# Sparse attention feeding a Sinkhorn-gated mixture of experts: the first batch's rounds with a step's values beside its transposes, eight rounds in place of nine, and half of the first weight pieces split inside the expert's first slots

## The chip, the cores and the metric

The kernel runs on one core of a Trainium2 chip. The metric is the device time of one execution in microseconds (us). Engines are named as in the profile: PE is TensorE (PEld its weight loads), DVE is VectorE, ACT is ScalarE, POOL is GpSimd, SP is the engine whose queue issues the DMAs.

## The reference, cut to what matters

```python
# attention: 4 batches, 8 heads, 576 positions, head_dim 64
scores = scale * q @ k.T
# heads 0..3: rel = i - j in 0..31;  heads 4..7: rel >= 0 and i % 32 == j % 32
attn = softmax(where(mask, scores, -1e9))        # rows divided by (sum + 1e-9)
x = (attn @ v) as [2304, 512]
# mixture of experts, E = 8, F = 1024
P = exp(x @ w_gate - max); 8 times: rows to 1, columns to 1, times N / E
out = sum over e of P[:, e:e+1] * (relu(x @ w1[e]) @ w2[e])
```

## The kernel before

**Attention in steps.** A batch of attention is eight steps: a pair of heads and a part of the positions. `STEPS` gives the order. Steps 0 to 3 of a batch are strided heads (in turn 4 and 6 blocks of scores, in two PSUM tiles, one for each head of the pair), steps 4 and 5 are local heads with four windows (positions 0 to 255), steps 6 and 7 local heads with five windows (positions 256 to 575). There are 32 steps. `at_k` counts rounds. A step k passes through four stages, each in another round:

- `at_scores` (line 195): score matmuls on PE, mask, scale and row minimum on DVE (L237), exponentials with row sums on ACT (L243).
- `at_normalize` (line 249): two short DVE instructions on the sums (L252, L253), then the multiplication on POOL (L255).
- `at_transpose` (line 259): transposes on PE (L267) into PSUM tiles of tag "t", then a DVE copy to `pt` (L268).
- `at_values` (line 271): values matmuls on PE (L280, L294), then for each piece the upper half of the result by ACT (L313) and the lower half by DVE (L314) into `reg`, the input x of the expert layers in two parts.

**Order.** The schedule is manual: each engine runs its instructions in the order in which the program emits them. Before the expert starts, nine rounds run for the first batch (lines 727 to 732). Round k emits scores of step k, values of step k - 3 (`LAG`), transposes of step k - 2, normalizing of step k - 1; the values round also issues the loads of step k + 2 on SP's queue. Rounds 1 to 8 each end with `split_w` of one weight piece: an ACT copy (L165), a POOL subtraction (L166), and the load of the next piece on SP's queue (four `raw` buffers). Four pieces are loaded ahead of the rounds.

**Slots.** Then the expert runs in slots (line 775): `layer1` of 256 tokens for a quarter of an expert's half (twelve PE matmuls, L389; relu on ACT and DVE, L395, L396) and `layer2` of the slot before (L413). As long as attention steps are left, a slot also holds one attention round, with the values in a PSUM tile of tag "t". `layer1` of slots 0 to 3 reads positions 0 to 255, so steps 0 to 5 of the first batch; slot 4 is the first that reads positions beyond them (steps 6 and 7). After the attention come gating, the second half of expert 0 and seven further experts (from about 250 us to the end).

```python
for k in range(2 * NP - 2 + LAG):
    attention_scores()
    attention_values("l1")
    attention_rest()            # transposes of at_k - 2, normalizing of at_k - 1
    if 1 <= k <= 2 * FH:
        split_w(*plain[k - 1])
```

Of the kernel before, what the change touches and what calls it, by code (L numbers as in the profile page):

```python
# [55 lines left out]
def kernel(  # L56
# [9 lines left out]
    nc = tc.nc  # L66
    P = 128
    NT, D = out.shape
    E, _, F = w1.shape
    NDT = D // P  # L70
    NP = NDT
    NTT = NT // P
    FH = 4
# [28 lines left out]
    cst = const.tile([P, 4, P], F32, name="cst")  # L102
# [45 lines left out]
    def load_w():  # L148
        nonlocal n_loaded
        if n_loaded == len(plain):  # L150
            return
        u, ft, which = plain[n_loaded]
        n_loaded += 1
        e, fh = divmod(u, UPE)
        f0 = (fh * FH + ft) * P
        t = raw_p.tile([P, D], F32, tag="raw", name=f"raw{which}_{u}_{ft}")
        if which == 0:
            t = t.rearrange("p (k f) -> p k f", f=P)
            nc.sync.dma_start(t, w1[e, :, f0 : f0 + P].rearrange("(k p) f -> p k f", p=P))
        else:  # L160
            load_w2(t, e, f0)
        raw[u, ft, which] = t
# [5 lines left out]
    def split_w(u, ft, which):  # L168
        src = raw.pop((u, ft, which))
        if which == 0:  # L170
            t = pools["w1"].tile([P, 2, NDT, P], F32R, tag="w1", name=f"w1_{u}_{ft}")
        else:
            t = w2_p.tile([P, 2, D], F32R, tag="w2", name=f"w2_{u}_{ft}")
        split(t[:, 0], t[:, 1], src)
        wt[u, ft, which] = t
        load_w()
# [5 lines left out]
    NS = len(steps)  # L182
    QK = -(-max(sum(_columns(*x)[:2]) for x in STEPS) // P) * P
    qkv_t, sms, sums_t, pts = {}, {}, {}, {}

    def load_qkv(k):
        if k < NS:
            nq, nk, nv = _columns(*steps[k][1:])
            t = pools["qkv"].tile([P, QK], F32, tag="qk", name=f"qk_{k}", bufs=3)
            nc.sync.dma_start(t[:, : nq + nk], qkv[k, :, : nq + nk])  # L190
            tv = pools["qkv"].tile([P, 5 * 2 * DH], F32, tag="v", name=f"v_{k}", bufs=5)
            nc.sync.dma_start(tv[:, :nv], qkv[k, :, nq + nk : nq + nk + nv])
            qkv_t[k] = t, tv[:, :nv].rearrange("p (w j d) -> p w j d", j=2, d=DH)
# [65 lines left out]
    def at_transpose(k):  # L259
        pts[k] = []  # L260
        for j, (sm, _, n, rows, nk) in enumerate(sms.pop(k)):
            pt = pools["qkv"].tile([P, 5, P], F32, tag="pt", name=f"pt_{k}_{j}", bufs=4)
            for i0 in range(0, n, 4):
                m = min(4, n - i0)
                tp = ps.tile([P, 4, P], F32, tag="t", name=f"tp_{k}_{j}_{i0}")
                for i in range(m):
                    nc.tensor.transpose(tp[:nk, i, :rows], sm[:, i0 + i, :], ident[:rows, :rows])  # L267
                nc.vector.tensor_copy(pt[:nk, i0 : i0 + m, :rows], tp[:nk, :m, :rows])  # L268
            pts[k].append((pt, n, rows, nk))

    def at_values(k, tag):
        b, p, hf = steps[k]
        tv = qkv_t.pop(k)[1]
        pv = ps.tile([P, 4 * P], F32, tag=tag, name=f"pv_{k}")
        if _is_local(p):
            ((pt, n, _, nk),) = pts.pop(k)
            ws = _windows(hf)
            for i, w in enumerate(ws):
                for j in range(2):
                    nc.tensor.matmul(  # L280
                        pv[DH * j : DH * j + DH, i * QT : (i + 1) * QT], tv[:nk, i, j, :],
                        pt[:nk, i, QT * j : QT * j + QT], start=True, stop=True,
                    )
            c0 = b * S + ws[0] * QT
            moves = [
                (pv[:, t - c0 : t - c0 + m], [xv(i, p, t, m) for i in range(2)])
                for t, m in pieces(c0, n * QT)
            ]
        else:
            r0, nr, n = SGROUPS[hf]  # L290
            m = nr * NJ
            for i in range(n):
                for j in range(2):
                    nc.tensor.matmul(  # L294
                        pv[DH * j : DH * j + DH, i * m : (i + 1) * m],
                        tv[:m, i, j, :], pts[k][j][0][:m, i, :m], start=True, stop=True,
                    )
            del pts[k]
            src = pv[:, : n * m].rearrange("p (r j) -> p j r", j=NJ)
            moves = [  # L300
                (
                    src[:, (t - b * S) // STRIDE : (t - b * S + m) // STRIDE, :],
                    [
                        xv(i, p, t, m).rearrange("p (j r) -> p j r", r=STRIDE)[
                            :, :, r0 : r0 + nr * n
                        ]
                        for i in range(2)
                    ],
                )
                for t, m in pieces(b * S, S)  # L310
            ]
        for src, (hi, lo) in moves:
            nc.scalar.activation(hi, src, AF.Copy)  # L313
            nc.vector.tensor_tensor(lo, src, hi.bitcast(F32), op=ALU.subtract)  # L314
        if k % len(STEPS) == len(STEPS) - 1:
            done.extend(c for c in range(NC) if b * S < min(NT, (c + 1) * CH) <= (b + 1) * S)
# [65 lines left out]
    def layer1(u, c, ft):  # L382
        c0, n = c
        ph = ps.tile([P, 4 * P], F32, tag="l1", name=f"ph_{u}_{c0}_{ft}")
        w = wt[u, ft, 0]
        k = 0
        for dt in range(NDT):
            for i, x in ((0, 0), (0, 1), (1, 0)):
                nc.tensor.matmul(  # L389
                    ph[:, :n], w[:, i, dt, :], xv(x, dt, c0, n),  # L390
                    start=(k == 0), stop=(k == 3 * NDT - 1),
                )
                k += 1
        h = pools["h"].tile([P, 2, 4 * P], F32R, tag="h", name=f"h_{u}_{c0}_{ft}")
        nc.scalar.activation(h[:, 0, :n], ph[:, :n], AF.Relu)  # L395
        nc.vector.scalar_tensor_tensor(  # L396
            h[:, 1, :n], ph[:, :n], 0.0, h[:, 0, :n].bitcast(F32), op0=ALU.max, op1=ALU.subtract
        )
        hs[u, c0, ft] = h
# [292 lines left out]

    LAG = 3
    at_k = 0

    def attention_scores():
        if at_k < NS:
            at_scores(at_k)

    def attention_rest():  # L700


        nonlocal at_k
        if 0 <= at_k - 2 < NS:
            at_transpose(at_k - 2)
        if 0 <= at_k - 1 < NS:
            at_normalize(at_k - 1)
        at_k += 1

    def attention_values(tag="t"):  # L710
        if at_k:
            store_x()
        if 0 <= at_k - LAG < NS:
            at_values(at_k - LAG, tag)
        if at_k:
            load_qkv(at_k + 2)

    load_qkv(0)
    nc.sync.dma_start(cst, consts)
    load_qkv(1)  # L720
    load_qkv(2)
    for _ in range(4):
        load_w()
    nc.sync.dma_start(wg_raw, wg.rearrange("(k p) e -> p k e", p=P))
    nc.gpsimd.memset(ones, 1.0)
    nc.gpsimd.memset(wgs.bitcast(F32), 0.0)
    for k in range(2 * NP - 2 + LAG):
        attention_scores()
        attention_values("l1")
        attention_rest()  # L730
        if 1 <= k <= 2 * FH:
            split_w(*plain[k - 1])
    for dt in range(NDT):
        c = 2 * E * dt
        nc.scalar.activation(wgs[:, c : c + E], wg_raw[:, dt, :], AF.Copy)
# [38 lines left out]
    prev = None  # L774
    for slot, (u, c, ft, last) in enumerate(slots):
        layer1(u, c, ft)
        if last and u + 1 < UPE:
            split_w(u + 1, ft, 0)
        busy = at_k < NS + LAG
        if busy:  # L780
            attention_values()
            attention_scores()
        if slot == len(slots) - 1:
            rest = [(prev[:3], None), ((u, c, ft), None)]
        elif prev is not None:
            pu, pc, pft, plast = prev
            layer2(pu, pc, pft)
            if plast and pu + 1 < UPE:
                split_w(pu + 1, pft, 1)
        if busy:  # L790
            attention_rest()
            if at_k == NS + LAG:
                store_x()
                stacks["right"].close()
                for name, bufs in (("sb", 1), ("hg", 8)):
                    pools[name] = ctx.enter_context(
                        tc.tile_pool(name=name, bufs=bufs, side="right")
                    )
                gat, s0 = gating(), sums(0)
                work = beside_second_half()  # L800
        else:
            next(gat, None)
            next(s0, None)
            for x in work.get(slot - len(slots) + 20, ()):
                x()
        prev = (u, c, ft, last)
    for x in (gat, s0):
        assert next(x, x) is x
# [99 lines left out]
```

## Time and profile before

| | |
|---|---|
| median of 3 runs | 1615.96 us (1615.15 to 4080.06) |
| profiled execution | 1614.86 us, of which the span is 1613.1 us |
| PE busy | 1597.0 us (99% of the span) |
| DVE, ACT, POOL busy | 936.1, 597.9, 957.1 us |
| chain that ended last | PE 97%, DVE 1%, ACT 1%, DMA 1% |
| first batch's nine rounds | about 0 to 37.3 us of the span |

The chain that ended last says which engine sets the time over the whole span. What happens in the first batch's rounds is read from that stretch alone: the busy times in windows, and the order of time on each engine.

### The profile page before, as it was taken

The page shows a single profiled execution, that of the slowest core. Times are in us where ns is not written, and L with a number is a line of the kernel's source. Part 1 is how long each engine was busy: PE and PEld are TensorE (multiplying, and loading weights), DVE is VectorE, ACT ScalarE, POOL GpSimd, SP SyncE. Part 2 cuts the span into 40 slices and gives each one's busy share as a digit, 9 for nine tenths or more (in the row PEclk, how much of TensorE's full clock was granted, in tenths as well). Part 3 has the DMA queues.
Part 4 walks back from the last instruction along what each step waited for, and adds up shares of the span by engine and source line. Part 5 has one row for each costly group of instructions (what it writes and reads, how often), then busy time and mean ns, then how long its engine had stood idle before and what let it go on. Part 6 is the DMA issues. An engine that isn't in the chain of part 4 may idle for free.

```text
span 1613.1 us, 24091 instructions
## 1 busy us (share of the span) xinstructions
PE 1597.0 (99%) x8779; PEld 1429.5 (89%) x8779; DVE 936.1 (58%) x1896; ACT 597.9 (37%) x1410; POOL 957.1 (59%) x874
## 2 busy tenths in 40 slices
PE   7999999999999999999999999999999999999999
PEld 5888888898989989899898998989989899898997
DVE  4665244466566665666666665666555665556655
ACT  6565222333333333343333433334333343333431
POOL 4222333287677766657767686765666656666562
PEclk9999999999999999999999999999999999999999
DMA  6553423432342223236222422322532222222221
GB/s 208 183 163 113 153 92 134 128 101 64 97 128 59 82 72 93 74 109 237 65 77 73 134 73 62 113 74 59 184 130 72 73 60 73 65 73 72 59 60 40
DMA packets 158296, 160.60 MB, mean 100 GB/s; under 512 B 11360, under 2 KB 122464, under 8 KB 158176
## 3 DMA queue, kind: packets, MB, share of 16 engines
q1 hardware_dynamic: 158176, 159.05, 32.2%
q8 instruction: 69, 1.13, 0.3%
q14 instruction: 51, 0.42, 0.1%
HBM read 135.41 MB, written 23.59 MB: 99 GB/s over the span
## 4 chain that ended last, share of the span: by engine, by line
PE 97%; DVE 1%; ACT 1%; DMA 1%; issue 0%; SPq 0%; POOL 0%; ACTq 0%; POOLq 0%; DVEq 0%
PE yg L596 43%; PE bb L581 16%; PE bc L581 11%; PE ba L581 11%; PE ph L389 6%; PE y L413 6%; PE tp L267 1%; PE sc L207 1%; PE pv L280 1%; ACT sm L243 1%; PE sc L224 1%; PE pl L323 1%; PE pv L294 0%; DMA v<-in_qkv 0%; DMA qk<-in_qkv 0%; DVE reg L314 0%
## 5 line engine op out<-in xcount | busy, mean ns | idle before, releaser
L596 PE MATMUL yg<-w2g,h 128*128 128x512 f32 x3024 | 702.8, 390 | 0.0
L596 PEld LDWEIGHTS yg<-w2g,h 128*128 128x128 f32 x3024 | 566.4, 188 | 115.1 <-DVE acc L603 0.4
L603 DVE SCALAR_TENSOR_TENSOR acc<-yg,gate,acc 128x512 f32<-128x512 f32 x504 | 378.4, 751 | 237.7 <-PE yg L596 237.5
L581 PE MATMUL bb<-reg 128*128 128x384 f32 x1512 | 304.9, 336 | 0.4 <-DVE h L396 0.4
L581 PEld LDWEIGHTS bb<-reg 128*128 128x128 f32 x1512 | 268.0, 188 | 7.2 <-DVE h L396 0.7
L166 POOL TENSOR_TENSOR reg<-rt,reg 128x512 fp32r<-128x512 f32 x83 | 115.9, 1397 | 233.1 <-ACT reg L165 233.1
L620 ACT ACTIVATE h<-m 128x384 fp32r<-128x384 f32 x84 | 44.2, 526 | 507.2 <-DVE m L616 507.2
L166 POOL TENSOR_TENSOR w2g<-r,w2g 128x512 fp32r<-128x512 f32 x168 | 213.6, 1293 | 22.8 <-ACT w2g L165 22.8
L166 POOL TENSOR_TENSOR reg<-ra,reg 128x512 fp32r<-128x512 f32 x83 | 107.3, 1293 | 163.7 <-ACT reg L165 163.7
L581 PE MATMUL ba<-reg 128*128 128x384 f32 x1008 | 201.7, 334 | 0.0
L581 PE MATMUL bc<-reg 128*128 128x384 f32 x1008 | 201.7, 334 | 0.0
L581 PEld LDWEIGHTS bc<-reg 128*128 128x128 f32 x1008 | 177.8, 188 | 0.0
L581 PEld LDWEIGHTS ba<-reg 128*128 128x128 f32 x1008 | 177.2, 188 | 0.1
L620 ACT ACTIVATE h<-u 128x384 fp32r<-128x384 f32 x168 | 88.3, 526 | 193.8 <-DVE u L616 193.8
L624 DVE SCALAR_TENSOR_TENSOR h<-ba,h 128x384 fp32r<-128x384 f32 x84 | 46.8, 558 | 162.9 <-ACT h L620 160.9
L616 DVE TENSOR_TENSOR u<-bc,u 128x384 f32<-128x384 f32 x168 | 93.7, 558 | 43.4 <-PE bc L581 40.5
L389 PE MATMUL ph<-reg,w 128*128 128x256 f32 (+1 forms) x672 | 114.2, 320 | 0.0
L616 DVE TENSOR_TENSOR u<-bb,m 128x384 f32<-128x384 f32 x168 | 93.7, 558 | 33.3 <-ACT reg L165 29.3
L413 PE MATMUL y<-w,h 128*128 128x512 f32 x432 | 110.6, 398 | 0.0
L553 POOL TENSOR_TENSOR rt<-rb,ra 128x512 f32<-128x512 f32 x83 | 107.4, 1294 | 4.1 <-DMA rb<-in_w 4.1
L166 POOL TENSOR_TENSOR reg<-ru,reg 128x512 fp32r<-128x512 f32 x83 | 107.0, 1289 | 2.3 <-ACT reg L165 2.3
L624 DVE SCALAR_TENSOR_TENSOR h<-u,h 128x384 fp32r<-128x384 f32 x168 | 101.9, 607 | 9.7
(82 smaller groups left out, 1467.2 us busy)
## 6 DMA issues: line engine op xcount, KB each, us to landing
r<-in_w SPq DMA_DIRECT2D x168, 256.0 KB, 2.9
ra<-in_w SPq DMA_DIRECT2D x166, 128.0 KB, 2.3
rb<-in_w SPq DMA_DIRECT2D x166, 128.0 KB, 2.3
sx<-xd SPq DMA_DIRECT2D x24, 384.0 KB, 5.8
sd<-so SPq DMA_DIRECT2D x24, 384.0 KB, 2.6
reg<-sd SPq DMA_DIRECT2D x12, 768.0 KB, 6.2
xd<-reg SPq DMA_DIRECT2D x4, 2048.0 KB, 7.9
reg<-xd SPq DMA_DIRECT2D x9, 768.0 KB, 5.5
```

What stands on the lines that cost most here:

```text
L166: nc.gpsimd.tensor_tensor(lo, src, hi.bitcast(F32), op=ALU.subtract)
L207: nc.tensor.matmul(sc[QT * j : QT * j + QT, i, :], t[sl, q0 : q0 + QT], t[sl, k0 : k0 + KW], start=True, stop=True,)
L224: nc.tensor.matmul(scs[j][:m, i, :m], t[sl, i * m : (i + 1) * m], t[sl, nq + i * m : nq + (i + 1) * m], start=True, stop=True,)
L389: nc.tensor.matmul(ph[:, :n], w[:, i, dt, :], xv(x, dt, c0, n), start=(k == 0), stop=(k == 3 * NDT - 1),)
L413: nc.tensor.matmul(y, h[:, a, i * P : (i + 1) * P], w[:, b, :], start=(ft == 0 and first), stop=(ft == FH - 1 and a == 1),)
L553: nc.gpsimd.tensor_tensor(t, b[:, 0:1, :].to_broadcast([P, 2, 2 * P]), a, op=ALU.subtract)
L581: nc.tensor.matmul(out[:, :TN], w[:, i, k, :], xops[x][:, xi, k, :], start=(start and n == 0), stop=(n == 5), skip_group_check=True,)
L596: nc.tensor.matmul(y, hg[g, i // 3, f][:, a, o : o + P], w2s[g][f][:, b, :], start=(f == 0 and a + b == 0), stop=(f == 1 and a == 1),)
L603: nc.vector.scalar_tensor_tensor(acc[:, t, :], y, gate[:, t, e : e + 1], acc[:, t, :], op0=ALU.mult, op1=ALU.add)
L616: nc.vector.tensor_tensor(o, bank[:, :TN], s, op=ALU.add)
L620: nc.scalar.activation(hg[g, i, f][:, 0], src[:, :TN], AF.Relu)
L624: nc.vector.scalar_tensor_tensor(h[:, 1], src[:, :TN], 0.0, h[:, 0].bitcast(F32), op0=ALU.max, op1=ALU.subtract)
```

## The change

The nine rounds become eight. A round now emits the transposes of step k - 2 first, then scores of step k, values of step k - 2 (lag 2 in place of 3), and normalizing of step k - 1. In the slots the lag is 3 as before, so slot 0 has no values; one further attention round is emitted at the end of slot 3, and from slot 4 on the order is that of before. A counter, `values_done`, keeps the values in order.

The constants' load goes ahead of the first step's v. The gate's weights and the first four weight pieces are loaded in rounds 1 to 4 and no longer ahead of the rounds. Of the eight first weight pieces four are split in rounds 6 and 7, two in each, and four in slots 0 and 1, two in each, behind `layer1`.

```diff
-    def attention_values(tag="t"):
+    def attention_values(tag="t", lag=LAG):
+        nonlocal values_done
         if at_k:
             store_x()
-        if 0 <= at_k - LAG < NS:
-            at_values(at_k - LAG, tag)
+        if 0 <= values_done <= at_k - lag < NS:
+            values_done += 1
+            at_values(at_k - lag, tag)
         if at_k:
             load_qkv(at_k + 2)
 
-    load_qkv(0)
-    nc.sync.dma_start(cst, consts)
+    load_qkv(0, [(cst, consts)])
     load_qkv(1)
     load_qkv(2)
-    for _ in range(4):
-        load_w()
-    nc.sync.dma_start(wg_raw, wg.rearrange("(k p) e -> p k e", p=P))
...
-    for k in range(2 * NP - 2 + LAG):
+
+    for k in range(2 * NP):
+        if 0 <= at_k - 2 < NS:
+            at_transpose(at_k - 2)
         attention_scores()
-        attention_values("l1")
-        attention_rest()
-        if 1 <= k <= 2 * FH:
-            split_w(*plain[k - 1])
+        attention_values("l1", 2)
+        at_normalize(at_k - 1) if at_k else None
+        at_k += 1
+        if k == 1:
+            nc.sync.dma_start(wg_raw, wg.rearrange("(k p) e -> p k e", p=P))
+        if 1 <= k <= 4:
+            load_w()
+        else:
+            for x in plain[:4][2 * (k - 6) : 2 * (k - 5)] if k > 5 else ():
+                split_w(*x)
+    late = list(plain[4 : 2 * FH])
...
         layer1(u, c, ft)
+        for _ in range(2 if slot < 2 else 0):
+            split_w(*late.pop(0))
         if last and u + 1 < UPE:
...
+        if slot == 3:
+
+            attention_values()
+            attention_scores()
+            attention_rest()
         prev = (u, c, ft, last)
```

## Rows read from the trace of the kernel before

**Rows 1.** Busy time of each engine in five windows: the nine rounds from the first DVE instruction to the first matmul of slot 0, then slots 0, 1, 2 and 3. Columns: window, its length, then busy us and count of instructions of PE, PEld, DVE, ACT, POOL, then granted TensorE clock (1.00 is 2.4 GHz, 0.50 is 1.2 GHz), DMA share, GB/s.

```profile
5.94:37.31 31.37, 25.11 (x217) 19.44 (x218) 18.12 (x117) 22.27 (x102) 16.22 (x18) 0.92 0.67 224
37.31:42.15 4.84, 4.62 (x50) 4.09 (x49) 3.00 (x15) 1.99 (x9) 2.43 (x3) 0.79 0.49 138
42.15:47.01 4.86, 4.86 (x52) 4.23 (x52) 3.83 (x27) 3.59 (x18) 1.17 (x2) 1.00 0.86 270
47.01:51.92 4.91, 4.91 (x47) 4.18 (x46) 3.27 (x22) 3.23 (x16) 1.41 (x2) 1.00 1.03 377
51.92:56.89 4.97, 4.97 (x54) 4.27 (x52) 2.93 (x15) 3.12 (x15) 1.17 (x2) 1.00 0.95 309
```

**Rows 2.** The order of time on DVE in the rounds: start us, us, engine and line, what it writes and reads, count. Shown are the first mask instruction of a round (L237), the first copy of transposes behind the round's values (L268) and the first instruction of normalizing (L252).

```profile
14.08 0.27 DVE L237 CUSTOM_DVE_ANT_0 sm<-sc,cst 108x108 f32<-108x108 f32 x1 [0.97 <-PE sc L224]
...
17.74 0.89 DVE L268 COPY pt<-tp 108x324 f32<-108x324 f32 x2
...
18.86 0.26 DVE L237 CUSTOM_DVE_ANT_0 sm<-sc,cst 128x96 f32<-128x96 f32 x1
...
21.86 0.74 DVE L268 COPY pt<-tp 126x252 f32<-126x252 f32 x2
22.52 0.16 DVE L252 TENSOR_SCALAR sums<-sums 108x6 f32<-108x6 f32 x1
...
22.83 0.26 DVE L237 CUSTOM_DVE_ANT_0 sm<-sc,cst 128x96 f32<-128x96 f32 x1
...
25.77 0.89 DVE L268 COPY pt<-tp 108x324 f32<-108x324 f32 x2
...
31.24 0.26 DVE L237 CUSTOM_DVE_ANT_0 sm<-sc,cst 128x96 f32<-128x96 f32 x1
...
34.16 0.68 DVE L268 COPY pt<-tp 96x512 f32<-96x512 f32 x1
...
37.77 0.88 DVE L268 COPY pt<-tp 96x512 f32<-96x512 f32 x2
```

**Rows 3.** The same view, earlier: the first mask instruction, held by the constants' load, and the first normalizing.

```profile
5.94 0.29 DVE L237 CUSTOM_DVE_ANT_0 sm<-sc,cst 126x126 f32<-126x126 f32 x1 [5.94 <-DMA cst<-in_consts]
...
9.50 0.17 DVE L252 TENSOR_SCALAR sums<-sums 126x4 f32<-126x4 f32 x1
```

**Rows 4.** The order of time on POOL: the multiplications of normalizing, one row for a step (strided with 4 and 6 blocks, local with 4 windows).

```profile
19.00 1.17 POOL L255 TENSOR_TENSOR sm<-sm,sums 126x252 f32<-126x252 f32 x2 [3.17 <-DVE sums L253]
...
23.07 1.42 POOL L255 TENSOR_TENSOR sm<-sm,sums 108x324 f32<-108x324 f32 x2 [1.68 <-DVE sums L253]
...
27.11 0.83 POOL L255 TENSOR_TENSOR sm<-sm,sums 128x384 f32<-128x384 f32 x1 [1.40 <-DVE sums L253]
```

**Rows 5.** The order of time on PE: scores (sc) and transposes (tp) of the rounds, then shapes of the slots (pv: values).

```profile
12.55 1.88 PE L224 MATMUL sc<-qk 64*108 64x108 f32 x12 [0.61 <-DMA qk<-in_qkv]
...
15.39 1.33 PE L267 MATMUL tp<-cst,sm 108*108 108x108 f32 x6
16.65 1.54 PE L207 MATMUL sc<-qk 64*64 64x96 f32 x16
...
19.95 1.10 PE L267 MATMUL tp<-cst,sm 126*126 126x126 f32 x4
...
32.35 1.00 PE L267 MATMUL tp<-cst,sm 128*96 128x128 f32 x4 [0.60 <-POOL sm L255]
...
51.43 0.72 PE L267 MATMUL tp<-cst,sm 108*108 108x108 f32 x6
...
56.54 0.59 PE L267 MATMUL tp<-cst,sm 126*126 126x126 f32 x4
...
58.49 0.65 PE L294 MATMUL pv<-pt,v 126*64 126x126 f32 x8
59.07 0.88 PE L207 MATMUL sc<-qk 64*64 64x96 f32 x16
...
66.64 0.60 PE L267 MATMUL tp<-cst,sm 128*96 128x128 f32 x4
...
69.22 1.04 PE L207 MATMUL sc<-qk 64*64 64x96 f32 x20
```

**Rows 6.** Busy time in windows of the rounds, columns as in rows 1. PE's busy time is the first number behind the length, the clock is the number behind POOL's.

```profile
30.00:33.00 3.00, 1.66 (x28) 1.25 (x24) 1.96 (x14) 2.08 (x10) 1.53 (x2) 0.92 0.68 217
33.00:36.00 3.00, 2.60 (x26) 1.86 (x24) 2.14 (x12) 1.82 (x9) 1.21 (x2) 0.50 0.47 127
...
39.00:42.00 3.00, 2.93 (x42) 2.37 (x41) 1.31 (x8) 0.99 (x3) 2.21 (x2) 0.95 0.73 206
```

**Rows 7.** The order of time on DVE in slot 3's beginning: the copy of a 6-block step's transposes and the normalizing behind it.

```profile
51.91 0.90 DVE L268 COPY pt<-tp 108x324 f32<-108x324 f32 x2 [0.16 <-PE tp L267]
52.73 0.16 DVE L252 TENSOR_SCALAR sums<-sums 126x4 f32<-126x4 f32 x1
```

**Rows 8.** Groups by line in the nine rounds: the exponentials on ACT, and the splits' instructions on POOL and ACT.

```profile
L243 ACT ACTIVATE sm<-sm,mx 128x96 f32<-128x96 f32 (+2 forms) x42 | 15.6, 373 | 11.1 <-DVE mx L237 11.1
L166 POOL TENSOR_TENSOR w<-raw,w 128x512 fp32r<-128x512 f32 x7 | 8.9, 1268 | 0.4 <-ACT w L165 0.4
...
L165 ACT ACTIVATE w<-raw 128x512 fp32r<-128x512 f32 x8 | 5.0, 619 | 0.0
```

**Rows 9.** DMA issues of the first 40 us by line: weight pieces, KB each, median us from issue to landing.

```profile
raw<-in_w SPq DMA_DIRECT2D x11, 256.0 KB, 2.9
```

More of the change, by code (lines that the diff above doesn't have):

```diff
@@ L184, with load_qkv @@
     qkv_t, sms, sums_t, pts = {}, {}, {}, {}
-    def load_qkv(k):
+    def load_qkv(k, more=()):
         if k < NS:
@@ L190, in load_qkv @@
             nc.sync.dma_start(t[:, : nq + nk], qkv[k, :, : nq + nk])
+            for x in more:
+                nc.sync.dma_start(*x)
             tv = pools["qkv"].tile([P, 5 * 2 * DH], F32, tag="v", name=f"v_{k}", bufs=5)
@@ L694 @@
     at_k = 0
+    values_done = 0
     def attention_scores():
```

## The prediction, made before the change ran

> **What bounds the kernel now.** Read the busy times first: PE is busy in 99% of the span and carries 97% of the chain that ended last. A change to the attention can therefore earn only where PE is not the limit, and the windows say where that is [rows 1]. In slots 1 to 3 PE is busy without a gap (4.86 of 4.86 us, 4.91 of 4.91, 4.97 of 4.97). In the nine rounds before them it is busy 25.1 of 31.4 us, part of that at half clock. So this stretch, about 37 us or 2.3% of the time, is the whole stake.
>
> Next, the order of time on DVE inside it [rows 2]. One round is a loop through DVE and ACT. The mask of step k starts (18.86); ACT follows with its exponentials, then splits the values of an older step with DVE, piece by piece; the DVE copy of transposes comes next (21.86), the normalizing (22.52), the mask of the next step (22.83). No PE or POOL work lies on this loop: 22.83 - 18.86 = 3.97 us a round. POOL's multiplication [rows 4] and the transposes that wait for it run during the *next* round's exponentials. This is what the old order buys with its ninth round: between normalizing a step and copying its transposes lies a whole DVE-ACT round.
>
> **The change, part by part.**
>
> *The rounds.* Every engine runs in program order (a DVE copy of transposes stands behind the older step's values [rows 2]), so the new order can be read from the code. DVE: copy(k-2), mask(k), values(k-2), normalize(k-1). PE: transposes(k-2), scores(k), values(k-2). At the end of a round normalizing starts only when the values are split; the next round's transposes stand at the *head* of PE's queue and need its product; the scores stand behind them, and the next mask needs both. So the path through POOL and PE, hidden until now, enters the loop: normalize on DVE, multiply on POOL, transpose, scores, mask. Queued behind PE's wait are the scores, and behind those DVE's mask and ACT's exponentials: nothing else in the round can run.
>
> I price it as two pieces. **D**, from a round's first mask to the end of its values' split, stays what it is; **G**, from there to the next first mask, is new.
>
> D from rows 2, mask to following copy, by round: round 4 (4 exponentials, values of 6 blocks) 21.86 - 18.86 = 3.00; round 5 (4, of 4 blocks) 25.77 - 22.83 = 2.94; round 7 (5, local) 34.16 - 31.24 = 2.92; round 3 (6, 4 blocks) 17.74 - 14.08 = 3.66. The new pairs: round 2 (4, 4 blocks) as round 3 less two exponentials of 0.37 [rows 8], 2.92; round 3 (6, 6 blocks) 3.66 + 0.06 = 3.72; rounds 4 and 5 are 2.94 and 3.00; 6 and 7 are 2.92 each. Sum 18.42.
>
> G = normalize to multiply + multiply + last transposes + scores to mask.
> - Normalize to multiply: 0.55 (22.52 to 23.07 [rows 2, 4]).
> - Multiply: 1.17 (4 blocks), 1.42 (6), 0.83 (local, 4 windows) [rows 4].
> - Transposes [rows 5]: of a strided step the second half is left, as the first half overlaps the multiplication. At the duration seen in the rounds: 1.10/2 = 0.55, 1.33/2 = 0.67, local 1.00. At that of the slots: 0.30, 0.36, 0.60.
> - Scores to mask: 14.08 - 12.55 = 1.53 for 6 blocks [rows 2, 5], two thirds of it, 1.02, for 4; local 1.54 + 0.13 = 1.67 with 16 matmuls, 20/16 of that work, 2.06, with 20. In the slots: half of the strided ones (0.77, 0.51), 0.88 + 0.13 = 1.01, 1.04 + 0.13 = 1.17.
>
> The copies (0.9 or less) run beside the scores. In the order of the six rounds, with the rounds' PE durations, G is 3.29, 4.17, 3.94, 4.31, 4.44, 4.44: sum 24.6. With the slots' durations: 2.53, 3.10, 3.03, 3.34, 3.15, 3.15: sum 18.3. In the kernel before the same distance was about 1.0 (21.86 to 22.83).
>
> *Which PE price?* At 30 to 33 us PE was busy 1.66 of 3 us, and from 33 us on the granted clock reads 0.50; it is back at 0.95 once PE is busy nearly without gap [rows 6]. In the new rounds PE has some 3.5 to 4.5 us of work in about 7, the same share, so I take the rounds' prices. The row 16.65 speaks for the same price early on: 16 score matmuls take 1.54 us there and 0.88 in slot 3 [rows 5], though the clock column of the page reads full speed at that time. The Trainium skill (TensorE: Matmul & The Clock Gate, What's actually happening) says that the throttled state is the default and activity releases it; by that rule the early rounds are at half clock, as these durations say and the column does not, and the sum stays at 24.6; by the column it would be 18.3.
>
> *Start and end of the rounds.* The first mask waits for the constants (5.94) and the first normalizing stands at 9.50 [rows 3]. The constants move up by one DMA issue, 0.46 us: I put the first normalizing at 9.0. The later place of weight loads removes at most the 0.61 us that scores(3) waited for qk [rows 5], a wait that no longer ends last. The split of step 5's values, which slot 0 needs, ends at 9.0 + 24.6 + 18.4 = 52.0, against 37.77 in the kernel before [rows 2]: **+14.2 us**. With the slots' PE prices 45.7, +7.9.
>
> *Splits.* In the rounds a split is an ACT copy of 0.62 us and a POOL subtraction of 1.27 us [rows 8]. Both lay in gaps, so taking them out earns nothing. Two in rounds 6 and 7 (1.24 and 2.54 us) lie behind the multiplication and in ACT's idle 4 us: nothing. In slots 0 and 1 they are different. POOL is free again about 2 x 2.54 us after the multiplication of slot 0, and step 7's multiplication queues behind them; ACT in slot 1 had 3.59 of 4.86 us of work [rows 1] and gets 1.24 more, and waits for pieces whose loads (2.9 us to landing [rows 9]) begin only when a buffer's split is done. A values tile held longer keeps the "t" tiles from the transposes. Between 0 (covered by PE's work) and 3; I take 0.7.
>
> *The further round in slot 3.* Slot 0 loses its values (-0.7), the further round adds values 0.65, scores 0.88, transposes 0.59 [rows 5], 2.1 in all, in a stretch where PE has no gap. Its values need the copy of transposes issued just before: these end at 51.43 + 0.72 = 52.15, the copy at 52.73 [rows 5, 7], a wait of some 0.7 that two neighbouring rounds always had a `layer1` to hide. Together -0.7 + 2.1 + 0.7 = 2.1, with the splits **+2.8 us**, between 1 and 5.
>
> Sum: 14.2 + 2.8 = 17.0. The profiled execution took 1614.86 us (span 1613.1), so 1631.9; the median of runs stands 1.1 above it: **1633**. Behind slot 4 nothing is changed and PE is the limit, so nothing is won back there.
>
> **The rivals.**
>
> *The clock holds.* PE stays at the slots' speed through the rounds: 7.9 + 2.8 = 10.7, so 1626.7. For it: the clock column still reads 0.92 at 30 to 33 us [rows 6]; against it the durations.
>
> *The loop does not lengthen; faster than before.* If normalizing's product is there in time (POOL early, or DVE not bound by the values), eight rounds keep the old pace: one round of 3.97 and about 1.1 of load waits go, 2.8 comes: -2.3, so 1613.7. It decides if less than about 1.3 us of G shows in a round. For it: POOL, DVE and ACT all have idle time in the rounds [rows 1]. Against: the idle time lies between instructions that depend on each other, and 0.55 + 0.83 alone is already more than that.
>
> *The late splits bind.* POOL's queue (six subtractions of 1.27, 7.6 us) and the late pieces hold the transposes of slots 0 to 2: up to 5 more, 1638.
>
> *Slower by over 2%.* The clock does not come back in the slots because their PE queue is broken up by these waits. Slots 1 to 3 take 14.74 us at clock 1.00 [rows 1]; at half they would cost about as much again, 1633 + 14.7 = 1648, and more if slot 4 is also caught. Against it: after the rounds before, the clock was back inside slot 0 [rows 1, 6].
>
> **How the numbers follow.** Forecast 60% (1629 to 1636), the clock holds 15%, faster 12%, late splits 10%, half clock in the slots 3%. The range 1622 to 1639 leaves out the faster case, the 3% and some tails: the bounds 7.9 + 1 to 14.2 + 5 (1624.9 to 1635.2), opened by the splits' rival above and by 3 below for the rows' coarseness. 2%, about what a measurement of this kernel can tell from no change, is 32 us, nearly the whole stretch: faster by over 2% would need it gone (0.01); slower by over 2% is the half clock in the slots (0.03).
>
> **What would show it.** In the changed kernel's DVE order, first masks should stand about 6.2 to 7.9 us apart from round 2 on, each with idle time ended by PE scores; PE's transposes should wait for POOL in each round; the split of step 5's values should end near 52 us, not 37.8; slot 3 should show values waiting for a copy. Rounds of 4 us would prove the loop reading wrong; rounds of 6 us with scores of 0.9 us would prove only the clock wrong. Slots 0 to 2 longer than 5.5 us would mean that the splits bind.

## The result and the profile after

| | before | after |
|---|---|---|
| median | 1615.96 us | 1634.23 us (1633.43 to 1634.58, 5 runs) |
| ratio after to before | | 1.0112, 95% interval 1.0099 to 1.0126 |
| profiled execution (span) | 1614.86 us (1613.1) | 1633.72 us (1632.0) |

The change costs 18 us, or 1.1%. (One run of before at 4080.06 us lies far outside and is left out of the ratio.) All of it falls ahead of slot 4: slot 4's first matmul stands at 75.76 us, where slot 3 of before ended at 56.89 [rows 1]. That is 18.87 us, and the span grew by 18.9. The interval of the ratio is about 0.13% wide on either side, so a change of 1.1% is clear of the noise; the 2% that the prediction takes as the limit of what can be told was too coarse.

Line numbers of the changed kernel are two higher inside the attention functions. The busy time in windows, columns as in [rows 1]: the rounds from the first mask to the matmul of slot 0 that needs step 5's values, then slots 0, 1, 2, and slot 3 with the further round.

```profile
4.79:53.03 48.24, 26.26 (x208) 19.79 (x208) 17.52 (x108) 18.28 (x89) 9.26 (x12) 1.00 0.43 127
53.03:56.77 3.74, 3.67 (x23) 3.03 (x23) 3.29 (x11) 2.80 (x9) 2.86 (x3) 0.70 0.13 45
56.77:62.59 5.82, 5.76 (x57) 4.89 (x56) 3.35 (x17) 3.67 (x13) 5.82 (x6) 0.90 0.66 188
62.59:67.42 4.83, 4.83 (x52) 4.20 (x52) 3.81 (x26) 3.68 (x18) 1.89 (x3) 1.00 0.93 282
67.42:75.76 8.34, 7.65 (x79) 6.04 (x78) 5.36 (x30) 5.01 (x24) 2.58 (x4) 1.00 1.04 391
```

There is one round less, yet the first stretch is 48.2 us long where it was 31.4. PE does 26.3 us of work in it in place of 25.1, so it is idle 22 us in place of 6. No other engine is busy more than 40% of it. This is a loop of waits, not load.

The order of time on DVE: first mask of a round (L239) and normalizing (L254), which follows the values' split.

```profile
9.27 0.16 DVE L254 TENSOR_SCALAR sums<-sums 126x4 f32<-126x4 f32 x1
...
12.88 0.29 DVE L239 CUSTOM_DVE_ANT_0 sm<-sc,cst 126x126 f32<-126x126 f32 x1 [0.72 <-PE sc L226]
...
15.88 0.16 DVE L254 TENSOR_SCALAR sums<-sums 108x6 f32<-108x6 f32 x1
...
20.16 0.27 DVE L239 CUSTOM_DVE_ANT_0 sm<-sc,cst 108x108 f32<-108x108 f32 x1 [0.96 <-PE sc L226]
...
28.00 0.26 DVE L239 CUSTOM_DVE_ANT_0 sm<-sc,cst 128x96 f32<-128x96 f32 x1 [1.17 <-PE sc L209]
...
35.61 0.26 DVE L239 CUSTOM_DVE_ANT_0 sm<-sc,cst 128x96 f32<-128x96 f32 x1 [1.10 <-PE sc L209]
...
38.62 0.16 DVE L254 TENSOR_SCALAR sums<-sums 128x4 f32<-128x4 f32 x1
...
43.08 0.26 DVE L239 CUSTOM_DVE_ANT_0 sm<-sc,cst 128x96 f32<-128x96 f32 x1 [1.23 <-PE sc L209]
...
50.45 0.26 DVE L239 CUSTOM_DVE_ANT_0 sm<-sc,cst 128x96 f32<-128x96 f32 x1 [1.23 <-PE sc L209]
...
53.35 0.16 DVE L254 TENSOR_SCALAR sums<-sums 128x5 f32<-128x5 f32 x1
```

Masks stand 7.28, 7.84, 7.61, 7.47 and 7.37 us apart, against about 4 before [rows 2]. Each of them waits for PE's scores. One whole round in the chain that ended last (start, us, what):

```profile
35.61 0.26 DVE sm L239
35.91 1.54 ACT sm L245 x8
37.45 0.30 ACT reg L315
37.78 0.47 DVE reg L316
38.27 0.21 ACT reg L315
38.50 0.20 DVE reg L316
38.70 0.09 DVE sums L254
38.81 0.19 DVE sums L255
...
39.16 0.83 POOL sm L257
40.04 1.09 PE tp L269 x4
41.13 1.82 PE sc L209 x20
...
43.08 0.26 DVE sm L239
```

The first six rows are the old loop; POOL, transposes and scores, from 39.16 to 42.95, are what joined it. The rest of the loss is in slot 3, on PE: the transposes of the slot's own round, then the further round (values, scores, transposes), then slot 4.

```profile
71.85 0.72 PE L269 MATMUL tp<-cst,sm 108*108 108x108 f32 x6
72.88 1.17 PE L296 MATMUL pv<-pt,v 108*64 108x108 f32 x12 [0.31 <-DVE pt L270]
73.98 0.88 PE L209 MATMUL sc<-qk 64*64 64x96 f32 x16
74.79 0.43 PE L269 MATMUL tp<-cst,sm 126*126 126x126 f32 x2
75.60 0.41 PE L269 MATMUL tp<-cst,sm 126*126 126x126 f32 x2 [0.38 <-DVE reg L316]
75.76 1.68 PE L391 MATMUL ph<-reg,w 128*128 128x256 f32 x12
```

The values wait for the copy, the second half of the transposes for DVE to release a "t" tile. Slot 3 takes 8.34 us where it took 4.97 [rows 1].

### The profile page after: what moved, and what is told of

Read it like the earlier page. It is cut to its first block, busy times and chain, and to the rows that moved or that the text cites. A ratio compares the mean times of both kernels' runs of the same rounds, so it can differ in the third digit from the quotient of the medians.

```text
span 1632.0 us, 24099 instructions
## 1 busy us (share of the span) xinstructions
PE 1600.7 (98%) x8779; PEld 1431.2 (88%) x8779; DVE 938.3 (57%) x1896; ACT 598.0 (37%) x1410; POOL 957.3 (59%) x874
## 4 chain that ended last, share of the span: by engine, by line
PE 97%; DVE 1%; ACT 1%; DMA 0%; POOL 0%; issue 0%; SPq 0%; POOLq 0%; DVEq 0%; ACTq 0%
PE yg L598 42%; PE bb L583 16%; PE bc L583 11%; PE ba L583 11%; PE ph L391 6%; PE y L415 6%; PE tp L269 1%; PE sc L209 1%; PE sc L226 1%; ACT sm L245 1%; PE pv L282 1%; PE pl L325 1%; PE pv L296 1%; DMA qk<-in_qkv 0%; POOL sm L257 0%; DVE reg L316 0%
## 5 line engine op out<-in xcount | busy, mean ns | idle before, releaser
L257 POOL TENSOR_TENSOR sm<-sm,sums 126x252 f32<-126x252 f32 (+3 forms) x48 | 35.2, 747 | 130.8 <-DVE sums L255 101.0
```

The source lines that it names most:

```text
L257: nc.gpsimd.tensor_tensor(sm, sm, rs.unsqueeze(2).to_broadcast([rows, n, nk]), op=ALU.mult)
```

## The experiments

Each kernel was timed beside runs of the kernel before; the ratios are to those. The theory is that POOL, transposes and scores joined the loop of a round (about 15 us), with a further 3 us in the slots. The rivals are the loads, the late splits, and PE's clock.

**The rounds alone.** The changed rounds and the further round, with loads and splits as before (the eighth split stands behind the last round).

```diff
+    for _ in range(4):
+        load_w()            # and wg_raw: ahead of the rounds, constants behind v
...
-        if 1 <= k <= 4:
-            load_w()
...
+        if k:
+            split_w(*plain[k - 1])
+    split_w(*plain[2 * FH - 1])
...
-        for _ in range(2 if slot < 2 else 0):
-            split_w(*late.pop(0))
```

> The changed kernel's eight rounds and further round in slot 3, with the loads and splits of the kernel before (four pieces and the gate's weights loaded ahead, one split in each round, none in the slots). Theory (the loop through POOL and PE is the loss): nearly the whole loss stays, 1632 to 1634 us; rounds 2 to 7 as far apart as in the changed kernel (7.3 us), and slot 1 back from 5.8 to about 4.9 us. Rival (the loads and late splits are the loss): 1616 to 1620 us.

Measured: 1634.85 us, ratio 1.0114 (1.0100 to 1.0128), a little over the 1632 to 1634 expected. The rounds carry the whole loss. First masks stand 7.2 to 7.8 us apart. Slot 1 did not come back to 4.9 but took 5.4 (58.67 to 64.10): its first twelve matmuls took 2.06 us, 1.68 in the next slot. By these durations PE was partly still at the lower clock, so the late splits are not the only thing that lengthens that slot.

**The loads and splits alone.** The old nine rounds with the changed loads, four splits in rounds 7 and 8 and four in slots 0 and 1.

```diff
-        if 1 <= k <= 2 * FH:
-            split_w(*plain[k - 1])
...
+        if 1 <= k <= 4:
+            load_w()
+        else:
+            for x in plain[:4][2 * (k - 7) : 2 * (k - 6)] if k > 6 else ():
+                split_w(*x)
+    late = list(plain[4 : 2 * FH])
...
+        for _ in range(2 if slot < 2 else 0):
+            split_w(*late.pop(0))
```

> The kernel before with the changed loads (constants ahead of v, gate's weights and weight pieces in rounds 1 to 4) and the changed splits (four in the last two rounds, four in slots 0 and 1); nine rounds in the old order. Theory: the rounds stay 4 us apart; the early load wait (0.6 to 2.2 us between rounds 2 and 3) goes, the late splits cost 0.7 to 1 in slots 0 and 1: 1614 to 1617 us. Rival (late splits hold the slots): 1620 us or more.

Measured: 1617.12 us, ratio 1.0007 (0.9998 to 1.0016); the profiled execution is the slowest of its runs, 1618.95. The rounds stay 4 us apart, and step 5's values are split at 36.4 us in place of 37.8. But slots 0 and 1 take 7.3 and 7.6 us there (4.8 and 4.9 before), so the late splits cost some 5 us in that execution. The medians say less: 1617.12 against 1614.49 with the same loads and no late splits (the fifth experiment), 2.6 us. Either way it is a miss of my 0.7 to 1. The chain that ended last shows how half of the 5 us came about:

```profile
34.88 2.52 POOL w L166 x2
...
37.41 3.70 DMA raw<-in_w
...
41.14 0.63 ACT w L165
41.77 0.28 ACT reg L315
...
42.79 0.23 DVE reg L316
...
43.16 0.29 PE tp L269
```

A weight piece can be loaded only when POOL's subtraction frees its buffer. ACT waits for the load, slot 0's values (L315) stand behind ACT's copy, and PE's last transpose waits for their "t" tile: 2.7 us of idle PE. The other half is PE's clock. In slot 1 (43.20 to 50.76) PE has no gap, but behind that idle stretch its granted clock reads 0.59 there on average, and its matmuls take longer:

```profile
43.16 0.29 PE L269 MATMUL tp<-cst,sm 128*96 128x128 f32 x1 [2.68 <-DVE reg L316]
...
47.33 2.93 PE L415 MATMUL y<-w,h 128*128 128x512 f32 x6
```

The same six matmuls take 1.65 us in slot 1 of before.

**Normalizing first.** One call moved in the changed kernel.

```diff
         attention_scores()
-        attention_values("l1", 2)
         at_normalize(at_k - 1) if at_k else None
+        attention_values("l1", 2)
```

> The changed kernel with one call moved: a round normalizes step k - 1 ahead of the values of step k - 2, so POOL's product and PE's transposes and scores run beside the exponentials again. Theory: first masks 3.8 to 4.7 us apart from round 3 on, in place of 7.3, step 5's values split by about 36 us in place of 53; with the slots' 3 us still paid, 1616 to 1618.5 us. Rival (PE's half clock or the merged values stage is the loss, not the place of normalizing): over 1625 us.

Measured: 1621.38 us, ratio 1.0034 (1.0021 to 1.0046); profiled execution 1619.40. This one line gives back 13 of the 18 us, so the place of normalizing behind the values is the main cause. It is a partial miss all the same: the time lies over the 1616 to 1618.5 expected, step 5's values are split at 39.3 us and not 36, and the masks of rounds 2 to 7 stand 5.1, 5.2, 5.5, 3.9 and 4.1 us apart. In rounds 2 to 4 the loop still runs through POOL and PE, from the round's last mask on:

```profile
18.60 0.18 DVE sm L239
18.78 0.09 DVE sums L254
18.90 0.19 DVE sums L255
...
19.22 0.61 POOL sm L257
19.84 0.04 issue
19.88 1.25 PE tp L269 x4
21.13 1.50 PE sc L209 x16
...
22.76 0.26 DVE sm L239
```

The transposes take 1.25 us and the scores 1.50, as in the rounds of before that ran at half speed [rows 5], and with those durations this way is longer than that by ACT. In rounds 6 and 7 the transposes take 0.64 us and the scores 1.04, as at full speed, and there the masks are 3.9 and 4.1 apart; so some of the 13 us came with the clock. Whether the clock decides it was left to the last experiment.

**PE filled.** Work for PE in its wait, to separate the clock from the loop.

```diff
+        if 2 <= k < 7:
+            fill = ps.tile([P, D], F32, tag="y", name=f"fill_{k}")
+            for _ in range(FILL):       # 10
+                nc.tensor.matmul(fill[:, :P], cst[:, 0, :], cst[:, 0, :], start=True, stop=True)
```

> The changed kernel with ten matmuls of the identity on itself behind the values of rounds 2 to 6, in PE's wait for POOL; their result is not read. Theory (the loop holds, PE's clock sets 6 of its 15 us): once PE is at 2.4 GHz the transposes take 0.6 to 0.7 and the scores 0.9 to 1.04, masks stand 6 us apart, 1628 to 1630.5 us. If the clock does not matter: 1634 us as before. If the fill does not raise the clock, it outlasts the wait by up to 0.8 us a round: 1636 to 1639 us.

Measured: 1628.51 us, ratio 1.0078 (1.0066 to 1.0091). On PE, from the end of round 5 to the scores of round 6, against 1.09 and 1.82 in the changed kernel's round above (each matmul of the fill makes two records, so ten show as x20):

```profile
33.40 2.50 PE L740 MATMUL fill<-cst 128*128 128x128 f32 x20
37.35 0.64 PE L269 MATMUL tp<-cst,sm 128*96 128x128 f32 x4 [1.45 <-POOL sm L257]
37.92 1.04 PE L209 MATMUL sc<-qk 64*64 64x96 f32 x20
```

Masks of rounds 5 to 7 now stand 6.2 and 6.1 us apart. So the half clock is some 6 us of the loss, and the loop itself and slot 3 (8.3 us here too) the rest: at 2.4 GHz a round is still 2 us longer than an old one.

**Early loads, nine rounds.** The load change without the late splits: the second experiment's kernel with all splits in rounds 3 to 8.

```diff
+        if k > 2:
+            for x in plain[max(k - 3, 2 * k - 10) : max(k - 2, 2 * k - 8)]:
+                split_w(*x)
```

> The kernel before, nine rounds in the old order, with the changed loads alone: constants ahead of v, gate's weights and four pieces loaded in rounds 1 to 4; all eight splits stay in the rounds (one each in rounds 3 to 6, two in 7 and 8). Theory (the loads gain 1.4 us at the start of the rounds, and the late splits alone ate it): step 5's values split near 36.4 us in place of 37.8, slots as in the kernel before, 1614 to 1615.2 us. If the late splits were not the reason, 1617 us as with them.

Measured: 1614.49 us, ratio 0.9993 (0.9984 to 1.0001). Its position agrees with a gain of about 1 us, though the interval still touches no change. Against the second experiment, which differs in four splits alone, it confirms that the late splits ate what the loads gave. One part is a miss: the values were split 1.3 us earlier, but slot 0 took 5.38 us in place of 4.84.

**Normalizing first, early splits.**

```diff
+        for x in plain[2 * (k - 4) : 2 * (k - 3)] if k > 3 else ():
+            split_w(*x)
...
-        for _ in range(2 if slot < 2 else 0):
-            split_w(*late.pop(0))
```

> The eight rounds with normalizing first, and all splits in rounds 4 to 7, two each, none in slots 0 and 1. Theory (late splits are mostly covered where slot 0 has no values; what is left is the further round in slot 3 and PE's half clock): 1619.5 to 1621.5 us, slots 0 to 2 at most 1 us shorter. Rival (late splits cost here what they cost beside the old rounds): 1616 to 1617.5 us.

Measured: 1620.99 us, ratio 1.0037 (1.0024 to 1.0051): no difference from the kernel with late splits. Slot 3 is 8.33 us there too (54.55 to 62.88).

**Early loads, PE filled.**

```diff
         attention_values("l1")
+        if 5 <= k <= 8:
+            fill = ps.tile([P, D], F32, tag="y", name=f"fill_{k}")
+            for _ in range(3):
+                nc.tensor.matmul(fill[:, :P], cst[:, 0, :], cst[:, 0, :], start=True, stop=True)
```

> The kernel with early loads and nine rounds, plus three matmuls of the identity on itself behind the values of rounds 5 to 8 (their result is not read), so that PE is at 2.4 GHz when slot 0 begins. Theory: the first twelve matmuls of the expert take 1.7 us in place of 2.5, slot 0 about 4.0 in place of 4.8: 0.5 to 1 us less than without the fill, 1613.3 to 1614.5 us. If the clock stays at half: no change, or 0.5 more.

Measured: 1613.01 us, ratio 0.9984 (0.9975 to 0.9993). This version beats both kernels, by 2.5 us over before. Slot 0's first twelve matmuls, with the early loads alone and then with the fill:

```profile
35.70 2.97 PE L391 MATMUL ph<-reg,w 128*128 128x256 f32 x12
```

```profile
35.81 2.26 PE L391 MATMUL ph<-reg,w 128*128 128x256 f32 x12
```

The rounds were 0.1 us later, slot 0 0.8 us shorter (4.59, 35.81 to 40.40, in place of 5.38). I had expected more, 1.7 for the twelve matmuls and 4.0 for the slot. The two profiled executions differ by 0.7 us, the medians by 1.5; where the other 0.8 lies is open.

**The changed kernel with early splits.** The same two edits as in the sixth experiment, made in the changed kernel.

> The changed kernel with all splits in rounds 4 to 7, two each, none in slots 0 and 1. The prediction's term for the late splits is 0.7 (0 to 3): 1633 to 1634.3 us. If they cost what they cost beside the old rounds (about 4): 1629.5 to 1630.5 us.

Measured: 1633.57 us, ratio 1.0112 (1.0098 to 1.0125). The ratio is that of the changed kernel, so the late splits cost nothing here that the medians can tell, where they cost 2.6 us beside the old rounds. In the profiles, from step 5's values to slot 4, it is 0.2 us (22.2 here, 22.4 in the changed kernel). The chain of the second experiment suggests why: slot 0 has no values here, so no "t" tile waits behind ACT's copy. No run separates that from the other differences.

**Normalizing first, PE filled.** The sixth experiment's kernel with a fill.

```diff
+        if 1 <= k < 7:
+            fill = ps.tile([P, D], F32, tag="y", name=f"fill_{k}")
+            for _ in range(8 if k == 1 else 4):
+                nc.tensor.matmul(fill[:, :P], cst[:, 0, :], cst[:, 0, :], start=True, stop=True)
```

> The eight rounds with normalizing first and early splits, plus matmuls of the identity on itself behind the scores of round 1 (eight) and the values of rounds 2 to 6 (four each; not read). In the kernel without them masks of rounds 2 to 5 stood 5.1 to 5.5 us apart, where the loop on DVE and ACT alone is 3.9 to 4.7. Theory (the loop is still mask, normalize, POOL, transposes, scores, and half of its PE part is the clock): with PE at 2.4 GHz from round 3 on the masks stand 4.0 to 4.7 apart, 1617 to 1619.5 us. If PE's clock is not in the loop: 1621 us as before.

Measured: 1618.00 us, ratio 1.0013 (1.0004 to 1.0022). From round 3 on masks stand 4.4 to 4.6 us apart:

```profile
17.10 0.27 DVE L239 CUSTOM_DVE_ANT_0 sm<-sc,cst 108x108 f32<-108x108 f32 x1 [0.34 <-PE sc L226]
...
25.97 0.26 DVE L239 CUSTOM_DVE_ANT_0 sm<-sc,cst 128x96 f32<-128x96 f32 x1 [0.43 <-PE sc L209]
```

Without the fill (the sixth experiment) they stand 5.1, 5.2, 4.7, 5.8 and 4.1 apart; the 5.5 in the text above is the third experiment's. So the clock was in that loop. With order and clock mended, eight rounds are still not faster than nine: step 5's values are split at 38.0 us, where the kernel before had them at 37.8, and slot 3 is still 8.33 us (51.68 to 60.01).

## Why the prediction was right

**The loop.** The step that carried it was the order of the queues: normalizing behind the values, transposes at the head of PE's queue. The chain shows exactly this sequence. By profiled executions the sum said 17.0 us and 18.9 came: the rounds cost 15.6 for 14.2 (the start 0.3, D 0.4 and G 0.7 more than forecast), the slots 3.3 for 2.8. Moving the one call gave back 13 us; undoing loads and splits gave back nothing measurable.

**D and G.** The six D sum to 18.8 us (predicted 18.4), the six G to 25.3 (24.6): for instance 15.88 to 20.16 is 4.28 (4.17), 38.62 to 43.08 is 4.46 (4.44). The largest miss is the first G, 3.61 for 3.29: from the start of the scores to the mask it takes 1.25 us with 4 blocks (11.63 to 12.88) and 1.56 with 6 (18.60 to 20.16), more than the two thirds that I took. In the strided rounds the transposes, not POOL, end last. They begin behind POOL's first half and take 1.24 to 1.47 us, as in the rounds of before at half clock, so "multiply plus half the transposes" fell short by 0.1 each.

**The start.** The first normalizing came at 9.27 (9.0). The constants no longer end the wait; the first mask, at 4.79, waited for scores.

**The clock's price.** The rounds' durations were the right choice: 7.3 to 7.8 us a round, not 6. The rival with the clock held is what the fourth experiment made: 1628.5, against its 1626.7.

**The slots.** Predicted +2.8. Measured: step 5's values are split at 53.35 and slot 4 begins at 75.76, 22.4 us, against 37.77 to 56.89, 19.1: +3.3. Slots 0 to 2 come to the same length as before (14.07 against 14.15 us), as -0.7 and +0.7 said. That they cancel so well is luck: without late splits (the eighth experiment) the three slots take 13.87 us, so by these profiles the two terms are nearer -0.3 and +0.2. The further round cost 3.4 for 2.8 (2.1 of work and 0.7 of waiting). The wait for the copy was right: 0.31 ahead of the values and 0.39 inside them, 1.17 us where the kernel before takes 0.78:

```profile
53.53 0.78 PE L294 MATMUL pv<-pt,v 108*64 108x108 f32 x12
```

But I took the values of a 4-block step, 0.65, where it is this 6-block step, and I left out the 0.38 for the "t" tile. The price of the late splits, 0.7, would have been short by 2 beside the old rounds.

**The other rivals.** Faster (1613.7) asked for less than 1.3 us of G in a round; G was 3.6 to 4.5. The clock was back within slot 1 (0.90 on average, 1.00 in slot 2), so the half clock did not reach the later slots. The late splits, which I had let cost up to 5 more, are answered by the eighth experiment.

## What to carry to other kernels

Before two stages of a pipeline are merged to save a round, follow what stands between them on every engine: a wait that was hidden for a whole round enters the loop if its result is needed at the head of the next one. In that case the place of a single producer in its queue, here two short instructions ahead of or behind the values, is worth more than the round. And a copy that waits for a load should not stand in a queue ahead of work that holds a PSUM tile.

## What the runs showed of the hardware

- In the rounds of the changed kernel the granted clock reads 1.00 throughout (4.79 to 53.03), while its instructions take what they take at the lower level: 20 score matmuls 1.87 us, against 1.04 in the slots. In the profile of the first experiment it reads 1.00 over the whole span, and yet nine matmuls of slot 0 take 2.53 us there, where twelve take 1.68 two slots on. Where the reading does fall, the durations agree: in the changed kernel it is 0.70 over slot 0, whose 8 score matmuls take 1.22 us (at 54.67) against 0.71 in slot 2. Ahead of the first change that a trace records, the duration of a known instruction says more than that column.
- PE can be brought to 2.4 GHz by work that nobody reads. In the fourth experiment the first fill of ten took 4.37 us and each later one 2.50, and from round 3 on the transposes between them were at full speed: 0.25 to 0.33 us for each one in rounds 3 to 5, against 0.38 to 0.47 in the changed kernel.
